# A decode block on one core: longer contiguous runs for K, V and w_down, and a softmax per chunk of keys in place of one per group

**Chip, cores, metric.** One core of one Trainium2 chip. All times are device microseconds of one execution; the kernel before takes 477 us. A program on one core has no second die to compare with, so I treat runs as comparable when they ran on the same chip in the same rounds.

## The reference

One token, model width 1024, everything in bf16:

```python
mod = silu(c) @ w_mod                      # 1024 x 6144 -> sa, ca, ga, sb, cb, gb
h = layernorm(x) * (1 + ca) + sa
x = x + ga * attention(h)                  # wq 1024x4096, 32 heads, 4 KV groups,
                                           # 65536 keys x 128, softmax, wo 4096x1024
h = layernorm(x) * (1 + cb) + sb
x = x + gb * ((gelu(h @ w_gate) * (h @ w_up)) @ w_down)   # 1024 -> 3584 -> 1024
```

What has to be loaded: w_mod 12.6 MB, wq 8.4, K and V 134.2, wo 8.4, gate and up 14.7, w_down 7.3: 185.6 MB in all, of which K and V are 72%.

## The kernel before

The engines go by their short names: PE is TensorE, DVE VectorE, ACT ScalarE, POOL GpSimd, and SP (SyncE) issues the loads. PSUM is the memory that PE writes.

K and V come in chunks of 8192 keys (2.097 MB), 8 chunks for each of the 4 groups, so 32 chunks of K and 32 of V. All loads are issued by SP, in one fixed order, into nine staging buffers of 2 MB; each load waits until PE has freed its buffer. For each K chunk PE transposes 128x128 blocks into PSUM, DVE and ACT take turns to evict them, and PE multiplies them with q. The scores of a whole group (65,536 keys) are kept, and the exponent waits for the group's maximum. V therefore follows K by LAG = 10 chunks. A step below is the work on one K chunk and one V chunk; a K-only step has no V chunk yet.

```python
E_KEYS = 16                                     # keys in one contiguous run: 16*128*2 B = 4 KB
CH = min(E_KEYS * P * 4, SK)                    # 8192 keys in a chunk
NA = CH // (P * E_KEYS)                         # 4 runs per partition
LAG = NCH + 2                                   # NCH = 8 chunks in a group
NKT = 8
NDD = 7                                         # row blocks of w_down in one load

def kv_src(tensor_ap, i):
    g, cch = divmod(i, NCH)
    return tensor_ap[0, g, cch * CH:(cch + 1) * CH, :].rearrange("(a p e) d -> p a (e d)", p=P, e=E_KEYS)
# ... cut ...
for st, (ki, vi) in enumerate(steps):           # order of the loads, vi = ki - LAG
    if ki is not None:
        ...                                     # K chunk, in kb0-kb2, wb0, wb1
    if vi is not None:
        addjob(("v", vi), f"vb{vi % 3}")        # V chunk, in three buffers
# ... cut: ACT, once per group ...
def emit_exp(g, h):
    if h == 0:
        wt(ac, s["dve"], ("negm_ready", g))     # the group's maximum
        wt(ac, sa, ("sccopied", g * NCH + NCH - 1))
    inst = ac.activation(out=PT[g % 2][:, h, :], in_=S[g % 2][:, h, :], func=ACT.Exp,
                         bias=negm[...], scale=SCALE, accum_out=sums[...])
# ... cut: PE ...
def emit_PV(vi, u):
    if u == 0:
        vbuf_t[vi] = job_begin(key)
        if cv == 0:
            wt(pe, s["exp"], ("exp_done", gv))  # first V chunk waits for the whole group
# ... cut: a buffer is freed by an instruction of its own ...
def job_end(key, inst=None):
    if inst is None:
        inst = pe.drain(fusable=True)
    rec(("free", key), b.fsem.inc(inst, 1))
```

Of the kernel before, what the change touches and what calls it, by code (L numbers as in the profile page):

```python
# [5 lines left out]
P = 128  # L6
# [6 lines left out]
E_KEYS = 16  # L13
STAGE_COLS = 8192

# [34 lines left out]
def bass_adaLN_cond__gqa_block_cached__geglu_ffn__decode_kernel(  # L50
# [26 lines left out]
    CH = min(E_KEYS * P * 4, SK)  # L77
    assert SK % CH == 0 and CH % (P * E_KEYS) == 0
    NA = CH // (P * E_KEYS)
    NB = NA * E_KEYS  # L80
# [3 lines left out]
    assert NCH >= 2  # L84
    NKC = G * NCH
    LAG = NCH + 2
    NSTEPS = NKC + LAG
    NKT = 8
    NTB = 4
    SLAG = 3  # L90
    SCALE = float(DH) ** -0.5
    EPS = 1e-5
    NBQ = SK // P
    WO_ROWS = HPG * DH
    NDD = 7
    assert CH <= STAGE_COLS

    with ExitStack() as es:
# [5 lines left out]
            "misc", "gp", "gpmx", "pe", "dve", "act", "t2act", "t2dve", "ea", "ed", "sdone", "scdone",  # L104
# [19 lines left out]
        S = [sb(f"S{j}", [P, HPG, NBQ], FP32) for j in range(2)]  # L124
        PT = [sb(f"PT{j}", [P, HPG, NBQ]) for j in range(2)]
# [16 lines left out]
        rmax = sb("rmax", [P, G * HPG], FP32)  # L142
        cmax = sb("cmax", [P, G * HPG], FP32)
        gmax = sb("gmax", [P, G * HPG], FP32)
        negm = sb("negm", [P, G * HPG], FP32)
        sums = sb("sums", [P, G * HPG], FP32)
# [18 lines left out]
        PVB = [pst("pv")]  # L165
        PR = [pst("pr")]
# [52 lines left out]
        pro_rot = ["kb0", "kb1", "kb2", "wb0", "wb1", "vb0", "vb1", "vb2"]  # L219
        kpool = ["kb0", "kb1", "kb2", "wb0", "wb1"]  # L220
# [10 lines left out]
        for st, (ki, vi) in enumerate(steps):  # L231
# [10 lines left out]
            if vi is not None:  # L242
                addjob(("v", vi), f"vb{vi % 3}")
                gq, cv = divmod(vi, NCH)
                if cv == WO_AT_CV:
                    addjob(("wo", gq), "wob")
                    s_last = v_step(gq * NCH + NCH - 1)
                    wo_step[gq] = (s_last + 2) if (s_last + 2) < NSTEPS else None
# [14 lines left out]
        pr_uses = []  # L263

        def prog_gp(gp):
# [9 lines left out]
            for g in range(G):  # L275
                wt(gp, s["dve"], ("rmax_ready", g))
                inst = gp.partition_all_reduce(gmax[:, g * HPG:(g + 1) * HPG], rmax[:, g * HPG:(g + 1) * HPG],
                                               P, bass.bass_isa.ReduceOp.max)
                rec(("gmax_ready", g), s["gpmx"].inc(inst, 1))

        def prog_sync(sy):
# [28 lines left out]
            for key, bname in jobs:  # L310
# [20 lines left out]
                elif kind == "down":  # L331
                    k0, k1 = down_jobs[key[1]]
                    src = B_w_down[k0 * P:k1 * P, :].rearrange("(ci p) n -> p ci n", p=P)
                    issue(key, lambda t, n=k1 - k0: t[:, 0:n * D].rearrange("p (ci n) -> p ci n", ci=n), src)
                else:
                    raise ValueError(key)
# [5 lines left out]
        def prog_pe(pe):  # L342
            pr = s["pr"]
            for b_ in BUFS.values():
                b_.consumed = 0

# [6 lines left out]
            def job_end(key, inst=None):  # L353
# [3 lines left out]
                if inst is None:  # L357
                    inst = pe.drain(fusable=True)
                rec(("free", key), b.fsem.inc(inst, 1))

            def pr_use(key):
                k = len(pr_uses)
                pr_uses.append(key)
                if k >= 1:
                    wt(pe, s["dve"], ("prfree", pr_uses[k - 1]))
                return 0, k

            def pr_done(key, inst=None):
                if inst is None:
                    inst = pe.drain(fusable=True)  # L370
                rec(("pr_ready", key), pr.inc(inst, 1))

            def matvec(prkey, lhs_fn, ncols, rhs_cols):
                bank, k = pr_use(prkey)
                last = None
                n = len(rhs_cols)
                for t in range(ncols):
                    for ci in range(n):
                        last = pe.matmul(PR[bank][:, t:t + 1], lhs_fn(ci, t), rhs_cols[ci],  # L379
                                         start=(ci == 0), stop=(ci == n - 1))  # L380
# [6 lines left out]
            inst = pe.matmul(PR[bank][:, 0:NI], x8[:, :], ident[0:NI, 0:NI], start=True, stop=True)  # L387
# [3 lines left out]
            inst = pe.matmul(PR[bank][:, 0:NI], silu8[:, :], ident[0:NI, 0:NI], start=True, stop=True)  # L391
# [9 lines left out]
            inst = pe.matmul(PR[bank][:, 0:1], ones_f[:, :], part1[:, 0:1], start=True, stop=True)  # L401
# [3 lines left out]
            inst = pe.matmul(PR[bank][:, 0:1], ones_f[:, :], part1[:, 1:2], start=True, stop=True)  # L405
# [7 lines left out]

            evac_done = {"act": s["ea"], "dve": s["ed"]}
# [5 lines left out]
            def emit_T(i, u):  # L420
# [5 lines left out]
                g, cch = divmod(i, NCH)  # L426
                tb = U % NTB
                ev = evac_engine(U)
                if U >= NTB:
                    Up = U - NTB  # L430
                    wt(pe, evac_done[evac_engine(Up)], ("evac_done", Up))
                last = None
                for bb in range(BU):
                    b = u * BU + bb
                    slot = blk_slot(b)
                    last = pe.matmul(TB[tb][:, bb * P:(bb + 1) * P], tt[:, slot:slot + P], ident[:, :],  # L436
                                     start=True, stop=True)
# [5 lines left out]
            def emit_S(i, u):  # L443
# [3 lines left out]
                if u == 0:  # L447
                    if i == 0:
                        wt(pe, s["dve"], "qT_ready")
                    if i >= 2:  # L450
                        wt(pe, s["act"], ("scfree", i - 2))
# [4 lines left out]
                for bb in range(BU):  # L456
                    b = u * BU + bb
                    last = pe.matmul(SC[scb][:, b * HPG:(b + 1) * HPG], kt[:, slot0 + bb * P:slot0 + (bb + 1) * P],  # L458
                                     qT[:, g * HPG:(g + 1) * HPG], start=True, stop=True)
                rec(("sdone", U), sdone.inc(last, 1))  # L460
                if u == NU - 1:
                    rec(("scdone", i), s["scdone"].inc(pe.drain(fusable=True), 1))  # L462
# [9 lines left out]
            def emit_PV(vi, u):  # L472
                key = ("v", vi)
                gv, cv = divmod(vi, NCH)
                if u == 0:
                    vbuf_t[vi] = job_begin(key)
                    if cv == 0:
                        wt(pe, s["exp"], ("exp_done", gv))
                        if gv >= 1:
                            wt(pe, s["dve"], ("pvfree", gv - 1))  # L480
                tt = vbuf_t[vi]
                last = None
                for bb in range(BU):
                    b = u * BU + bb
                    bq = cv * NB + b
                    slot = blk_slot(b)
                    first = (cv == 0 and b == 0)
                    final = (cv == NCH - 1 and b == NB - 1)
                    last = pe.matmul(PVB[0][:, 0:HPG], tt[:, slot:slot + DH], PT[gv % 2][:, :, bq],  # L489
                                     start=first, stop=final)  # L490
                if u == NU - 1:
                    job_end(key)
                    if cv == NCH - 1:
                        rec(("pv_done", gv), s["pv"].inc(pe.drain(fusable=True), 1))

            def group_tot(gv):
                wt(pe, s["exp"], ("exp_done", gv))
                bank, k = pr_use(("tot", gv))
                inst = pe.matmul(PR[bank][:, 0:HPG], ones_f[:, :], sums[:, gv * HPG:(gv + 1) * HPG],  # L499
                                 start=True, stop=True)  # L500
                pr_done(("tot", gv), inst)

            def group_wo(gv):
# [3 lines left out]
                bank, k = pr_use(("woacc", gv))  # L507
                last = None
                for t in range(NI):
                    for hl in range(HPG):  # L510
                        last = pe.matmul(PR[bank][:, t:t + 1],  # L511
                                         tt[:, hl * D + t * P:hl * D + (t + 1) * P],
                                         oT[:, gv * HPG + hl:gv * HPG + hl + 1],
                                         start=(hl == 0), stop=(hl == HPG - 1))
# [33 lines left out]

            wt(pe, s["dve"], "ln2_part1_ready")
            bank, k = pr_use("ln2_sum1")  # L550
            inst = pe.matmul(PR[bank][:, 0:1], ones_f[:, :], part1[:, 2:3], start=True, stop=True)
# [3 lines left out]
            inst = pe.matmul(PR[bank][:, 0:1], ones_f[:, :], part1[:, 3:4], start=True, stop=True)  # L555
            pr_done("ln2_sum2", inst)
            wt(pe, s["dve"], "h2T_ready")
            for kind in ("gate", "up"):
                for j2 in range(NI // 2):
                    key = (kind, j2)  # L560
                    tt = job_begin(key)
                    matvec((kind, j2), lambda ci, t, tt=tt: tt[:, ci * F + t * P:ci * F + (t + 1) * P],
# [3 lines left out]
            for jd, (k0, k1) in enumerate(down_jobs):  # L566
# [4 lines left out]
                job_end(key)  # L571
            wt(pe, s["dve"], "outT_ready")
            bank, k = pr_use("outT")
            inst = pe.matmul(PR[bank][0:NI, 0:P], outT_b[:, :], ident[:, :], start=True, stop=True)
            pr_done("outT", inst)

        def prog_dve(dv):
# [4 lines left out]

            def prbank(key):
                return PR[0]
# [106 lines left out]
            def chunk_max(i):  # L691
                g, cch = divmod(i, NCH)
                wt(dv, s["act"], ("sccopied", i))
                chain_wait()
                if cch == 0:
                    target = rmax[:, g * HPG:(g + 1) * HPG]
                else:
                    target = cmax[:, g * HPG:(g + 1) * HPG]
                inst = dv.tensor_reduce(out=target, in_=S[g % 2][:, :, cch * NB:(cch + 1) * NB], axis=AX.X,  # L699
                                        op=ALU.max)  # L700
                done(inst)
                if cch > 0:
                    chain_wait()
                    inst = dv.tensor_tensor(out=rmax[:, g * HPG:(g + 1) * HPG], in0=rmax[:, g * HPG:(g + 1) * HPG],
                                            in1=target, op=ALU.max)
                    done(inst)
                if cch == NCH - 1:
                    rec(("rmax_ready", g), sd.count)

            def group_negm(g):  # L710
                wt(dv, s["gpmx"], ("gmax_ready", g))
                inst = dv.tensor_scalar(out=negm[:, g * HPG:(g + 1) * HPG], in0=gmax[:, g * HPG:(g + 1) * HPG],  # L712
# [258 lines left out]
```

## Time and profile before

| | us |
|---|---|
| median of 16 runs (beside those of the changed kernel) | 477.05 |
| lowest to highest | 475.95 to 481.90 |
| span of the profiled execution | 476.0 |
| mean granted clock of TensorE | 0.713 |

The lines themselves are in the prediction below. The page cuts the span into 40 slices of 11.9 us and gives for each the busy share of every engine in tenths, the granted clock of TensorE and what the DMA engines moved. A table of stretches gives the same counters between two times of one's choice. Read the DMA share together with GB/s: a full share at a low rate means that the transfers themselves are slow; a low share means that some engines had nothing left to carry, mostly because nothing was queued.

### The profile page before, as it was taken

The numbers are of one execution on the slowest core, as the hardware profiler recorded it, in microseconds if no ns is written. First come the engines' busy times: TensorE is split into PE (matmuls) and PEld (weight loads), VectorE is DVE, ScalarE is ACT, GpSimd is POOL, SyncE is SP. The second block draws the span as 40 slices with busy tenths as digits, with TensorE's granted clock in tenths as the row PEclk, the third lists the DMA queues.
The fourth block names the chain that finished last, engine by engine and source line by source line (L and its number), as shares of the span: only waits on it lengthen the run. The fifth ranks groups of instructions, "written<-read, shape, count | busy, mean of one in ns | idle before, by whom it ended". The sixth has DMA issues, their size and how long they took to land.

```text
span 476.0 us, 17150 instructions
## 1 busy us (share of the span) xinstructions
PE 341.9 (72%) x7731; PEld 322.6 (68%) x7731; DVE 210.8 (44%) x400; ACT 207.0 (43%) x361; POOL 2.3 (0%) x11
## 2 busy tenths in 40 slices
PE   0445398888598989989889988999989553164242
PEld 0344287777498989988879988899979442154232
DVE  0002078888476675545465565445755000020010
ACT  2000077787965565675355567545655500010000
POOL 0000000000000000000000000000000000000000
PEclk9999999999788685556585575565887555555555
DMA  8999999999989999999999999999998999999994
GB/s 316 423 421 421 410 408 407 406 410 406 408 346 352 394 407 398 407 408 408 407 408 407 400 405 407 408 409 390 399 368 305 412 409 405 404 418 418 409 386 159
DMA packets 46201, 186.71 MB, mean 392 GB/s; under 512 B 1584, under 2 KB 1584, under 8 KB 44080
## 3 DMA queue, kind: packets, MB, share of 16 engines
q1 hardware_dynamic: 46128, 185.61, 98.1%
q8 instruction: 61, 1.00, 0.9%
q14 instruction: 12, 0.10, 0.1%
HBM read 185.60 MB, written 0.00 MB: 390 GB/s over the span
## 4 chain that ended last, share of the span: by engine, by line
PE 38%; issue 23%; DMA 20%; SPq 8%; ACT 6%; DVE 3%; PEldq 0%; PEld 0%; POOLq 0%; POOL 0%; DVEq 0%; ACTq 0%
PE tb L436 23%; SPq L297 8%; PE sc L458 7%; PE pv L489 6%; DMA vb<-in_w_mod_dram 6%; DMA vb<-in_A_v_cache_dram 6%; DMA kb<-in_B_w_down_dram 4%; DMA kb<-in_A_k_cache_dram 4%; ACT PT L883 3%; ACT kt L862 3%; DVE kt L688 1%; DVE cmax L699 1%; PE pr L511 1%; PE pr L379 1%; ACT L883 0%
## 5 line engine op out<-in xcount | busy, mean ns | idle before, releaser
L688 DVE CAST kt<-tb 128x512 bf16<-128x512 f32 x256 | 174.9, 690 | 109.8 <-PE tb L436 109.5
L862 ACT ACTIVATE kt<-tb 128x512 bf16<-128x512 f32 x256 | 151.6, 600 | 128.9 <-PE tb L436 126.6
L489 PE MATMUL pv<-PT,vb 128*128 128x8 bf16 x2048 | 119.8, 180 | 34.9 <-DMA vb<-in_A_v_cache_dram 20.8
L489 PEld LDWEIGHTS pv<-PT,vb 128*128 128x128 bf16 x2048 | 111.6, 111 | 41.5 <-DMA vb<-in_A_v_cache_dram 23.0
L458 PE MATMUL sc<-qT,kt 128*128 128x8 bf16 x2048 | 126.7, 167 | 18.1 <-ACT kt L862 8.3
L436 PE MATMUL tb<-ident,kb 128*128 128x128 bf16 x1152 | 132.0, 254 | 7.3 <-DMA kb<-in_A_k_cache_dram 4.2
L458 PEld LDWEIGHTS sc<-qT,kt 128*128 128x128 bf16 x2048 | 95.6, 100 | 24.3 <-ACT kt L862 11.2
L436 PE MATMUL tb<-ident,wb 128*128 128x128 bf16 x704 | 90.7, 275 | 1.4 <-issue 0.3
L436 PEld LDWEIGHTS tb<-ident,kb 128*128 128x128 bf16 x1152 | 81.0, 110 | 9.5 <-DMA kb<-in_A_k_cache_dram 4.3
L436 PEld LDWEIGHTS tb<-ident,wb 128*128 128x128 bf16 x704 | 54.4, 118 | 2.5 <-issue 2.0
L872 ACT ACTIVATE S<-sc 128x512 f32<-128x512 f32 x32 | 33.8, 1058 | 4.7 <-PEq L462 4.2
L883 ACT ACTIVATE PT<-S,negm 128x512 bf16<-128x512 f32 x32 | 22.6, 709 | 1.6 <-DVE negm L712 1.6
L920 ACT ACTIVATE stat<-stat 128x1 f32<-128x1 f32 x1 | 0.2, 203 | 47.3 <-DVE stat L643 47.3
L718 DVE RECIPROCAL rtot<-pr 128x8 f32<-128x8 f32 x4 | 0.8, 208 | 43.2 <-PE pr L499 43.2
L699 DVE TENSOR_REDUCE cmax<-S 128x8 f32<-128x512 f32 x28 | 18.9, 676 | 2.3 <-ACT S L872 2.3
L436 PE MATMUL tb<-ident,vb 128*128 128x128 bf16 x192 | 16.3, 217 | 0.3
L850 ACT ACTIVATE stat<-stat 128x1 f32<-128x1 f32 x1 | 0.2, 203 | 35.3 <-DVE stat L643 35.3
L923 ACT ACTIVATE ff<-ff 128x28 f32<-128x28 f32 x1 | 0.2, 226 | 29.3 <-DVE ff L810 29.3
L379 PE MATMUL pr<-h2T,vb 128*128 128x1 bf16 x168 | 5.0, 165 | 9.5 <-DMA vb<-in_B_w_up_dram 9.5
L436 PEld LDWEIGHTS tb<-ident,vb 128*128 128x128 bf16 x192 | 11.1, 96 | 0.6 <-issue 0.6
L379 PE MATMUL pr<-ffT,kb 128*128 128x1 bf16 x168 | 5.0, 165 | 9.0 <-DMA kb<-in_B_w_down_dram 9.0
L616 DVE TENSOR_TENSOR modacc<-modacc,pr 128x48 f32<-128x48 f32 x7 | 1.4, 204 | 22.5 <-PE pr L379 22.5
(103 smaller groups left out, 126.2 us busy)
## 6 DMA issues: line engine op xcount, KB each, us to landing
vb<-in_A_v_cache_dram SPq DMA_DIRECT2D x32, 2048.0 KB, 13.3
kb<-in_A_k_cache_dram SPq DMA_DIRECT2D x18, 2048.0 KB, 21.8
wb<-in_A_k_cache_dram SPq DMA_DIRECT2D x11, 2048.0 KB, 22.5
wob<-in_A_wo_dram SPq DMA_DIRECT2D x4, 2048.0 KB, 17.9
vb<-in_A_k_cache_dram SPq DMA_DIRECT2D x3, 2048.0 KB, 25.4
kb<-in_B_w_gate_dram SPq DMA_DIRECT2D x3, 1792.0 KB, 20.1
vb<-in_B_w_up_dram SPq DMA_DIRECT2D x3, 1792.0 KB, 29.9
kb<-in_B_w_down_dram SPq DMA_DIRECT2D x3, 1792.0 KB, 20.6
```

What stands on the lines that cost most here:

```text
L297: inst = sy.dma_start(dst_fn(b.t), src_ap)
L379: last = pe.matmul(PR[bank][:, t:t + 1], lhs_fn(ci, t), rhs_cols[ci], start=(ci == 0), stop=(ci == n - 1))
L436: last = pe.matmul(TB[tb][:, bb * P:(bb + 1) * P], tt[:, slot:slot + P], ident[:, :], start=True, stop=True)
L458: last = pe.matmul(SC[scb][:, b * HPG:(b + 1) * HPG], kt[:, slot0 + bb * P:slot0 + (bb + 1) * P], qT[:, g * HPG:(g + 1) * HPG], start=True ...
L489: last = pe.matmul(PVB[0][:, 0:HPG], tt[:, slot:slot + DH], PT[gv % 2][:, :, bq], start=first, stop=final)
L511: last = pe.matmul(PR[bank][:, t:t + 1], tt[:, hl * D + t * P:hl * D + (t + 1) * P], oT[:, gv * HPG + hl:gv * HPG + hl + 1], start=(hl == ...
L616: inst = dv.tensor_tensor(out=modacc[:, :], in0=modacc[:, :], in1=prbank(("mod", i))[:, 0:NT_MOD], op=ALU.add)
L688: inst = dv.tensor_copy(kt[:, slot0:slot0 + BU * P], TB[tb][:, 0:BU * P])
L699: inst = dv.tensor_reduce(out=target, in_=S[g % 2][:, :, cch * NB:(cch + 1) * NB], axis=AX.X, op=ALU.max)
L862: inst = ac.activation(out=kt[:, slot0:slot0 + BU * P], in_=TB[tb][:, 0:BU * P], func=ACT.Copy)
L872: inst = ac.activation(out=out_ap, in_=in_ap, func=ACT.Copy)
L883: inst = ac.activation(out=PT[g % 2][:, h, :], in_=S[g % 2][:, h, :], func=ACT.Exp, bias=negm[:, g * HPG + h:g * HPG + h + 1], scale=SCALE ...
```

## The change

Its intent is to make the loads faster and to keep them coming. Cut to the core:

```diff
-    CH = min(E_KEYS * P * 4, SK)
-    NA = CH // (P * E_KEYS)
-    NB = NA * E_KEYS
+    CH = min(CHUNK_KEYS, SK)          # 8192, as before
+    E_KEYS = CH // P                  # 64 keys in a run: 16 KB
+    NA = 1
+    NB = E_KEYS
-    LAG = NCH + 2
+    LAG = 3
-    NKT = 8
+    NKT = 6
-    NDD = 7
+    NDD = 8
-    kpool = ["kb0", "kb1", "kb2", "wb0", "wb1"]
+    kpool = ["kb0", "kb1", "kb2", "wb0"]
+    vpool = ["vb0", "vb1", "vb2", "wb1"]
 # w_down: eight rows of 2 KB that follow each other in memory go to one partition, 16 KB in a run
-    src = B_w_down[k0 * P:k1 * P, :].rearrange("(ci p) n -> p ci n", p=P)
+    src = B_w_down[k0 * P:k1 * P, :].rearrange("(p ci) n -> p (ci n)", ci=k1 - k0)
 # so gate and up must deliver their columns in that order: stationary reads with a step of n elements
+    def ff_cols(tt, ci, t):
+        n = k1 - k0
+        lo = ci * F + k0 * P + (t - k0)
+        return tt[:, lo:lo + (P - 1) * n + 1:n]
 # softmax per chunk: maximum from PSUM, all-reduce, x - max with a transposing write, exp, sum
+    def chunk_max(i):      dv.tensor_reduce(rmax[i], SC[i % 2] as "p h b", max)
+    def chunk_negm(i):     dv.tensor_scalar(negm[i], gmax[i], -1.0)       # after POOL's all-reduce
+    def chunk_sc_copy(i):  dv.tensor_tensor(SR[i % 2] as "p b h", SC[i % 2], negm[i], add)
+    def emit_exp(i, h):    ac.activation(PTR[i % 4], SR[i % 2], Exp, scale=SCALE)
+    def chunk_psum(i):     dv.tensor_reduce(sums[i], PTR[i % 4], add)
 # ... cut: group_post weights the 8 chunks of a group by exp(their max - the group's max) and adds them
 # PE: free a buffer with an increment on the next matmul, no drain
     def job_end(key, inst=None):
-        if inst is None:
-            inst = pe.drain(fusable=True)
-        rec(("free", key), b.fsem.inc(inst, 1))
+        definc(b.fsem, ("free", key), inst)      # waits in a list until the next mm()
```

Small matrix-vector results now rotate over the PSUM banks GB and TB instead of using one bank.

## The prediction

> **What bounds the kernel now.** I read the page's slices first, then the DMA queues, then the same counters over chosen stretches, then the order of time inside one step. The slices:
>
> ```profile
> PE   0445398888598989989889988999989553164242
> PEclk9999999999788685556585575565887555555555
> DMA  8999999999989999999999999999998999999994
> GB/s 316 423 421 421 410 408 407 406 410 406 408 346 352 394 407 398 407 408 408 407 408 407 400 405 407 408 409 390 399 368 305 412 409 405 404 418 418 409 386 159
> DMA packets 46201, 186.71 MB, mean 392 GB/s; under 512 B 1584, under 2 KB 1584, under 8 KB 44080
> ```
>
> The DMA row is full from end to end, and 186 MB in 476 us is nearly all that this core moves at its best slice (423 GB/s). So the transfers set the time. PE reads 9 in the middle, but there it runs at half clock. Two things in this view are worth money: the rate differs between stages although DMA is equally "busy" in each, and there are dips (slices 12-13 and 28-31). I then asked for the stretches one by one; columns are stretch, length, busy us of PE, PEld, DVE, ACT, POOL, clock, DMA share, GB/s:
>
> ```profile
> 12.00:36.00 24.00, 10.14 (x346) 9.60 (x342) 1.43 (x7) 0.00 (x0) 0.00 (x0) 1.00 1.01 423
> 108.00:120.00 12.00, 10.36 (x231) 9.36 (x227) 10.29 (x18) 9.68 (x16) 0.00 (x0) 1.00 1.02 408
> 140.00:144.00 4.00, 3.68 (x96) 3.39 (x93) 3.09 (x6) 2.14 (x5) 0.00 (x0) 1.00 0.38 132
> 264.00:276.00 12.00, 11.79 (x218) 11.44 (x216) 6.89 (x11) 6.18 (x11) 0.00 (x0) 0.50 1.04 400
> 364.00:368.00 4.00, 3.43 (x101) 3.10 (x99) 1.91 (x3) 2.54 (x4) 0.00 (x0) 1.00 0.55 177
> 372.00:418.00 46.00, 17.70 (x579) 16.76 (x579) 0.54 (x3) 4.98 (x13) 0.00 (x0) 0.50 1.03 407
> 426.00:444.00 18.00, 9.38 (x330) 9.02 (x326) 0.92 (x5) 0.00 (x0) 0.00 (x0) 0.50 1.01 418
> 456.00:468.00 12.00, 4.54 (x159) 4.40 (x159) 0.33 (x3) 0.00 (x0) 0.00 (x0) 0.50 1.04 384
> ```
>
> At a full share the rate is 423 while w_mod loads (12 KB contiguous per partition), 418 for gate and up (7 KB), 407 to 408 for K and V (4 KB), 384 for w_down (2 KB). The rate follows the run length, not the engines: 372 to 418 has PE at 38% and still 407. The two starved stretches are 140 to 144 (all buffers full: the first group's softmax had to wait for eight chunks of K) and 364 to 368.
>
> **What the Trainium skill says.** "DMA: Bandwidth & Descriptors", section "Why small descriptors are slow (HBM only)", names a fixed overhead per packet. The trace agrees: one fixed cost fits all four rates. An engine carries 1/16 of the rate: 12288 B take 465 ns at 423, 4096 B take 160.6 ns at 408. The difference gives 0.0371 ns per byte and 8.5 ns per packet; from these 7 KB should run at 417 (418 seen) and 2 KB at 388 (384 seen). The same page, "Where 436 GB/s comes from", puts the ceiling at 435; my fit's limit for endless runs is 431. "Advanced Engine Details and Errata", section "SBUF Cachelines", says that an access to a new 16-byte line each time pays a penalty. The change makes the stationary reads of gate and up step by 16 bytes. No stationary operand of the kernel before is strided, so its trace says nothing here. "TensorE: Matmul & The Clock Gate", "What's actually happening", gives two clock states, 4/8 and 8/8; the stretches above at 0.50 and 1.00 agree.
>
> **The change part by part.** (1) *Longer runs.* K and V chunks go from 16 keys (4 KB) to 64 keys (16 KB) per partition in one run; w_down's rows are regrouped so that eight 2 KB rows become one 16 KB run. By the fit a 16 KB packet takes 8.5 + 608 = 617 ns, 425 GB/s. K and V are 64 x 2.097 = 134.2 MB: 329.0 us at 408, 315.8 at 425, so 13.2 us less. w_down is 7.34 MB: 19.1 us at 384, 17.3 us at about 424 (its last job has 8 KB runs), 1.8 us less. As DMA is the bound, both count in full: -15.0 us.
>
> (2) *Softmax per chunk instead of per group.* Each chunk of 8192 keys gets its own maximum, exponent and sum, combined at the group's end, so V follows K by 3 steps and not by 10. The long K-only lead that fills all buffers and then starves the queue disappears, and so does the end where the last group's exponents hold everything back. Lost now, measured against 407 GB/s: 136 to 148 lose 0.25 + 2.7 + 0.45 = 3.4 us; 328 to 332, 344 to 348 and 364 to 368 lose 0.5 + 0.5 + 2.3 = 3.3 us. Of these 6.7 us I give 2 to new waits: -4.7 us.
>
> (3) *What it adds, beside the path if the engines have room.* DVE per chunk now: eight evictions at 0.69, one maximum of 0.68 and 0.17 = 6.4 us. After: 8 x 0.69, a maximum straight from PSUM (estimate 0.7), negation 0.17, the subtraction that writes with a stride (estimate 1.1, because ACT's strided copy of the same 128x512 takes 1.06 against 0.60 for a plain one), a sum of 0.68: 8.2 us. ACT loses the 1.06 copy and the accumulator reads (0.19 each): 8 x 0.60 + 0.71 = 5.5 us. The all-reduce on POOL takes 0.37 us, 32 times instead of 4, with one eviction between request and use. A step of one K and one V chunk takes DMA 2 x 2.097 MB / 425 = 9.9 us, so DVE at 8.2 stays hidden. Only the three first K-only steps will run at DVE's pace, about 8 us each; eight staging buffers cover that.
>
> (4) *PE.* Same matmuls. In the order of time at half clock one unit (4 transposes, 4 of PV, 4 scores) repeats every 0.64 us:
>
> ```profile
> 257.54 0.69 DVE L688 CAST kt<-tb 128x512 bf16<-128x512 f32 x1 [0.47 <-PE tb L436]
> 257.56 0.59 PE L436 MATMUL tb<-ident,wb 128*128 128x128 bf16 x4
> 257.94 0.30 PE L489 MATMUL pv<-PT,vb 128*128 128x8 bf16 x4
> 258.09 0.25 PE L458 MATMUL sc<-qT,kt 128*128 128x8 bf16 x4
> 258.20 0.59 PE L436 MATMUL tb<-ident,wb 128*128 128x128 bf16 x4
> ```
>
> 16 x 0.64 = 10.24 us a step; the output projection adds 1.9 us in 8 steps: 10.5 us. DMA per step after: 9.87 + one 2.097 MB load of wo per 8 steps at 388 GB/s, 0.68: 10.55 us. So at half clock PE has just enough room, at full clock plenty. The drains that now signal freed buffers and finished scores (bubbles of 0.2 to 0.4 us two or three times a step) are replaced by an increment on the next matmul, which is what makes 10.24 reachable.
>
> (5) *End.* From the last landing to the end now takes 4.75 us; the chain shows where it begins:
>
> ```profile
> 452.72 18.53 DMA kb<-in_B_w_down_dram
> 471.30 1.66 PE pr L379 x56
> 472.99 0.17 DVE down_acc L828
> ```
>
> w_down goes from 4 x 7 to 8 + 8 + 8 + 4 row blocks, so the last job has 32 matmuls instead of 56, at 29.5 ns each: -0.7 us. The rotation of PSUM banks frees PE from waiting for each small eviction; with DMA the bound that is worth nothing.
>
> Sum: 477.2 - 15.0 - 4.7 - 0.7 = 456.8, say **457 us**.
>
> **The rivals.** *PE or DVE becomes the bound.* For it: margin at half clock is 0.05 us a step, and DVE's new strided work may delay evictions that PE needs. Against it: before runs at 0.62 mean clock in the middle, not 0.50, and four PSUM banks give PE 2.5 us of slack. If a step took 11.0 us, 29 steps would be 319 against 306 us, less about 5 us of lead: some 465 us. *The rate does not follow the run length* (16 KB no better than 4 KB): then only parts 2 and 5 remain, 472 us, "same". Against it: four rates on one line, two of them not used for the fit. *Strided weight loads in gate and up.* 448 weight loads, now about 29.5 ns each (56 in 1.65 us). They have from h2T, about 10 us after the last V chunk lands (416.2 to 425.7 now), until the weights end 52 us after it; less 4 us for the activation chain and 6 us for the first three down jobs this leaves 32 us, 71 ns per matmul. Twice as slow (59 ns) is still hidden; at 90 ns it adds 8 us (465), at four times some 21 us (478). Nothing in the profile decides between these; I give over 71 ns a chance of one in five.
>
> **Range and chances.** The rivals reach 465 from two sides, and a few us of stall that I keep might vanish (452); a fit limit of 431 leaves little below 449. Range 449 to 468. 2% faster is 467.7: only a failed rate gain or a fourfold weight load miss it. Faster 0.84, within 2% 0.13, slower 0.03.
>
> **What would show it.** Part 1: K and V stretches at 422 to 426 GB/s with a full share, packets down from 46201 to about 18,500 (24,576 fewer for K and V, 3,072 fewer for w_down). Part 2: no slice under 380 before the last. Part 3: per-step DVE near 8.2 us, subtraction near 1.1, DVE idle mostly on PE. Part 4: PE idle on DMA of K or V, not on DVE. Part 5: the chain ends with a w_down landing. I am wrong if the rate stays at 408 with a full share, if the DMA share falls in the middle with PE at 98%, or if gate and up loads run over 71 ns each and the chain's end goes through them.

## The result

| | median us | lowest to highest | runs | clock of the profiled run |
|---|---|---|---|---|
| before | 477.05 | 475.95 to 481.90 | 16 | 0.713 |
| after | 458.23 | 457.93 to 458.48 | 11 | 0.761 |

The ratio is 0.9591 (95% interval 0.9567 to 0.9615): faster by 4.1%, 19.5 us of 477. Here and below a ratio is the mean time of one kernel's runs over that of the other's of the same rounds, so it is not quite the ratio of the medians. Executions over 1.5% slower than the fastest of the same kernel are left out of the means. Predicted were 457.0 us; the median is 1.2 us above.

The changed kernel is not only faster but steadier: its 11 runs lie within 0.55 us, the 16 runs before within 6.

The page of the changed kernel, cut to five of its lines; each slice is now 11.4 us:

```profile
PE   1335378888888398888968799887588888659754
PEclk9999999987787658867676959687677867555555
DMA  7999999999999999999999999999999999999992
GB/s 306 419 424 421 426 429 423 420 428 426 421 422 409 428 424 426 420 426 428 406 420 430 422 422 429 425 413 414 424 428 425 424 426 364 412 419 418 425 384 104
DMA packets 18553, 186.71 MB, mean 409 GB/s; under 512 B 1584, under 2 KB 1584, under 8 KB 7728
```

From the fifth to the thirty-third slice the rate is now what it was only under w_mod before. The two deep dips (346, 352 and 368, 305) are gone; small ones stay (409, 406, 413), and one of 364. The packets fell by 27,648, just the 24,576 of K and V and 3,072 of w_down that the prediction counted, and the bytes are the same.

Stretches of the changed kernel (stretch, length, busy us of PE, PEld, DVE, ACT, POOL, clock, DMA share, GB/s):

```profile
60.00:120.00 60.00, 50.58 (x1144) 48.15 (x1142) 49.12 (x81) 37.26 (x63) 2.22 (x6) 0.91 1.01 424
148.00:320.00 172.00, 142.22 (x3167) 138.58 (x3164) 119.08 (x209) 83.49 (x145) 5.84 (x16) 0.74 1.01 422
384.00:388.00 4.00, 2.46 (x46) 2.46 (x46) 1.98 (x4) 1.65 (x3) 0.00 (x0) 0.63 0.91 352
440.00:446.00 6.00, 2.84 (x100) 2.77 (x101) 0.50 (x3) 0.00 (x0) 0.00 (x0) 0.50 0.74 313
446.00:456.00 10.00, 4.04 (x131) 3.60 (x127) 1.27 (x7) 0.00 (x0) 0.00 (x0) 0.50 0.24 95
```

K and V run at 424 early and at 422 over the whole middle, wo included, with a full share. PE has 142 busy us in 172, so it waits. The last two lines show something that the prediction has not: the share falls to 0.74 from 440 on although every load has been issued. I come back to it.

The groups (line, engine, operation, count, busy us, mean ns, idle time before and its cause), then the waits (us in total, times, longest):

```profile
L764 DVE CAST kt<-tb 128x512 bf16<-128x512 f32 x256 | 172.4, 685 | 95.5 <-PE tb L493 94.7
L786 DVE TENSOR_TENSOR SR<-sc,negm 128x512 f32<-128x512 f32 x32 | 33.1, 1034 | 0.1
```

```profile
PE gb L366 <- DMA wb<-in_A_v_cache_dram: 19.0, 5, 4.5
PE gb L366 <- DMA vb<-in_A_v_cache_dram: 12.7, 8, 3.2
PE sc L366 <- DVE kt L764: 4.5, 9, 1.2
```

PE waits 31.7 us for V to land and only 4.5 us for an eviction by DVE. DVE in turn is idle for 95 us, because PE has no new transposes for it. The end of the chain of work that ended last, in order of time (start, us, what):

```profile
415.47 3.11 PE gb L366 x55
418.71 33.60 DMA kb<-in_B_w_down_dram
452.36 0.99 PE tb L366 x31
```

The last w_down load lands at 452.35; 4.1 us later the kernel is over (4.75 before). Gate's strided matmuls are on the inferred chain, but from 418.71 on it is the landing that counts.

### The profile page after: what moved, and what is told of

It reads as the page before. It is cut to its first block, busy times and chain, and to the rows that moved or that the text cites. A ratio compares the mean times of both kernels' runs of the same rounds, so it can differ in the third digit from the quotient of the medians.

```text
span 456.5 us, 17156 instructions
## 1 busy us (share of the span) xinstructions
PE 337.5 (74%) x7731; PEld 327.1 (72%) x7731; DVE 253.4 (56%) x488; ACT 176.8 (39%) x301; POOL 12.6 (3%) x39
## 4 chain that ended last, share of the span: by engine, by line
DMA 49%; PE 31%; SPq 11%; DVE 4%; issue 4%; ACT 1%; DVEq 0%; ACTq 0%
DMA wb<-in_A_v_cache_dram 31%; PE tb L366 15%; SPq L314 11%; DMA kb<-in_B_w_down_dram 7%; DMA wb<-in_w_mod_dram 7%; PE gb L366 6%; DMA kb<-in_A_k_cache_dram 4%; PE tb L493 4%; PE sc L366 4%; PE sc L516 1%; PE gb L546 1%; DVE kt L764 1%; DVE rmax L770 1%; DVE SR L786 0%; ACT kt L967 0%
## 5 line engine op out<-in xcount | busy, mean ns | idle before, releaser
L366 PE MATMUL tb<-ident,kb 128*128 128x128 bf16 x1152 | 153.4, 256 | 11.2 <-DMA kb<-in_A_k_cache_dram 8.3
L366 PE MATMUL sc<-qT,kt 128*128 128x8 bf16 x1536 | 112.7, 167 | 12.5 <-issue 5.5
L366 PE MATMUL gb<-PTR,vb 128*128 128x8 bf16 x1152 | 90.9, 180 | 15.8 <-DMA vb<-in_A_v_cache_dram 12.7
L493 PE MATMUL tb<-ident,kb 128*128 128x128 bf16 x384 | 100.7, 262 | 0.0
L366 PEld LDWEIGHTS gb<-PTR,vb 128*128 128x128 bf16 x1152 | 79.9, 110 | 17.9 <-DMA vb<-in_A_v_cache_dram 14.3
L366 PEld LDWEIGHTS sc<-qT,kt 128*128 128x128 bf16 x1536 | 78.7, 99 | 14.9 <-issue 5.6
L366 PEld LDWEIGHTS tb<-ident,kb 128*128 128x128 bf16 x1152 | 79.0, 107 | 11.7 <-DMA kb<-in_A_k_cache_dram 8.6
L516 PE MATMUL sc<-qT,kt 128*128 128x8 bf16 x512 | 85.3, 167 | 0.0
L546 PE MATMUL gb<-PTR,vb 128*128 128x8 bf16 x384 | 65.1, 175 | 2.1 <-issue 2.0
L516 PEld LDWEIGHTS sc<-qT,kt 128*128 128x128 bf16 x512 | 50.7, 99 | 3.0 <-issue 3.0
L493 PEld LDWEIGHTS tb<-ident,kb 128*128 128x128 bf16 x384 | 46.9, 122 | 0.3 <-issue 0.3
L366 PE MATMUL gb<-PTR,wb 128*128 128x8 bf16 x384 | 31.2, 183 | 19.5 <-DMA wb<-in_A_v_cache_dram 19.0
L366 PEld LDWEIGHTS gb<-PTR,wb 128*128 128x128 bf16 x384 | 29.6, 120 | 20.7 <-DMA wb<-in_A_v_cache_dram 20.3
L546 PEld LDWEIGHTS gb<-PTR,vb 128*128 128x128 bf16 x384 | 37.9, 99 | 0.1
L786 DVE TENSOR_TENSOR SR<-sc,negm 128x512 f32<-128x512 f32 x32 | 33.1, 1034 | 0.1
L366 PEld LDWEIGHTS tb<-ident,wb 128*128 128x128 bf16 x384 | 25.1, 103 | 2.0 <-issue 2.0
```

The source lines that it names most:

```text
L366: inst = pe.matmul(*args, **kwargs)
L493: last = f(TB[tb][:, bb * P:(bb + 1) * P], tt[:, slot:slot + P], ident[:, :], start=True, stop=True)
L516: last = f(SC[scb][:, b * HPG:(b + 1) * HPG], kt[:, slot0 + bb * P:slot0 + (bb + 1) * P], qT[:, g * HPG:(g + 1) * HPG], start=True, stop=True)
L546: last = f(GB[gv % 2][:, cv * HPG:(cv + 1) * HPG], tt[:, slot:slot + DH], PTR[vi % NPR][:, :, b], start=first, stop=final)
L786: inst = dv.tensor_tensor(out=out_ap, in0=in_ap, in1=negm_b, op=ALU.add)
```

## The experiments

a_run4k, b_run16k, a_olddown and a_drains ran on one chip (before: 477.91 us median); a_lag6, a_3plus3, a_nostride_wrong and a_stride4 (before 478.66); a_gates2, a_gates3_ndd4, a_run8k and a_fetch (before 478.81). Each ratio is to the kernel before on the same chip. All ran, and all were correct except the one that is wrong on purpose. Where two kernels are set against each other, I take the difference of these ratios times 477 us; a ratio's interval is some 2 us to either side, so differences of 1 or 2 us are estimates.

### Does the run length make the rate? a_run4k and a_run8k

The changed kernel with only the run length of K and V set back to 4 KB, or to 8 KB with 32 in place of 16:

```diff
-    E_KEYS = CH // P
-    NA = 1
-    NB = E_KEYS
+    E_KEYS = 16
+    NA = CH // (P * E_KEYS)
+    NB = NA * E_KEYS
```

> The changed kernel with one thing undone: K and V are again read in runs of 4 KB per partition (16 keys) instead of 16 KB (64 keys); softmax per chunk, buffers, w_down stay as changed. Theory (the rate follows the run length): K and V stretches fall from 424 to about 408 GB/s at a full DMA share, the time rises by 134.2 MB/408 - 134.2 MB/424 = 12.4 us, to about 470.6 us (ratio to the kernel before 0.986). Rival (the higher rate comes from the deeper queue and the missing K-only lead, not from the runs): rate stays near 422, time 458 to 460 us (ratio 0.96).

> The changed kernel with K and V in runs of 8 KB, a third point for the cost of a packet. From 8.5 ns per packet and 0.0371 ns per byte on each engine: 419 GB/s in K and V stretches, 134.2 MB/419 - 134.2 MB/425 = 4.5 us more than with 16 KB, 462.7 us. If the cost were not per packet but a threshold between 4 and 16 KB, the time would be at either end, 458 or 471.6 us.

4 KB: 471.61 us (4 runs, 471.45 to 471.75), ratio 0.9862 [0.9808, 0.9916]. 8 KB: 462.76 us (4 runs, 462.54 to 462.86), 0.9669 [0.9636, 0.9702]. The same stretch as above, first at 4 KB, then at 8 KB:

```profile
60.00:120.00 60.00, 52.03 (x1124) 49.47 (x1125) 48.11 (x79) 36.53 (x62) 2.23 (x6) 0.86 1.03 407
```

```profile
60.00:120.00 60.00, 50.97 (x1144) 48.33 (x1144) 49.18 (x81) 37.27 (x63) 2.22 (x6) 0.91 1.01 419
```

The share is full in all three and the rate is 407, 419, 424. The prediction's line (0.0371 ns per byte and engine, 8.5 ns per packet) was drawn through 4 KB and 12 KB; at 8 KB it gives 8192 B in 312.4 ns, 16 engines 419.6 GB/s, and 419 was measured. So the run length alone is worth 0.0271 of 477 us between 4 KB and 16 KB: 12.9 us.

### Are long runs enough? b_run16k

The kernel before with 16 KB runs and nothing else, so with its group softmax, its LAG of 10 and its drains:

```diff
-E_KEYS = 16
+E_KEYS = 64
-    CH = min(E_KEYS * P * 4, SK)
+    CH = min(E_KEYS * P, SK)
```

> The kernel before with one thing done: K and V in runs of 16 KB per partition; softmax per group of eight chunks, buffers and w_down as before. Theory: rate in K and V stretches 424 GB/s; 12.6 us less if all of it counts, 464.5 us (ratio 0.974); but the K-only lead runs at 6.9 us a chunk on PE, DVE and ACT whatever the DMA does, so the queue starves earlier and longer after it and 2 to 4 us are given back: 465 to 468 us. Together with a_run4k this makes a two by two table; if the parts simply add, (before - a_run4k) is what the new softmax and w_down bring alone, about 6 us. Rival (run length without effect): 476 to 478 us.

474.73 us (14 runs, 470.53 to 480.75, one of them slow), ratio 0.9913 [0.9882, 0.9944]: 4.2 us, not the 9 to 12 that I expected. The rate is there, 424 GB/s from 60 to 120 us, but the queue runs dry for longer. Stretches, and SP's issues in order of time (start, us, what):

```profile
140.00:144.00 4.00, 4.00 (x85) 4.00 (x83) 2.78 (x6) 2.02 (x4) 0.00 (x0) 0.59 0.00 0
144.00:148.00 4.00, 3.79 (x103) 3.53 (x100) 2.81 (x5) 2.89 (x6) 0.00 (x0) 1.00 0.39 86
```

```profile
122.07 0.33 SPq L297 DMA_DIRECT2D kb<-in_A_k_cache_dram  x1
145.61 0.33 SPq L297 DMA_DIRECT2D vb<-in_A_v_cache_dram  x1
```

SP issues a K chunk at 122.07 and then nothing for 23.5 us, because the next V buffer is not free before the first group's softmax is done and the first V chunk consumed. In the kernel before the same hole lies between 121.50 and 142.67. The eight buffers that hold K and V (wob takes no K or V) last less long when they arrive faster, and PE, which has to end the wait, is no faster: it is busy all through these 8 us, in part at half clock. Over 132 to 148 and 328 to 372 us this run moves 164 and 352 GB/s and so loses 9.8 and 7.5 us against 424. Over the same two stretches the kernel before moves 321 and 362 GB/s and loses 3.4 and 4.9 us against 407 (the 6.7 of the prediction count only some pieces of them). That is 9 us more, enough to account for what the long runs did not bring (12.9 - 4.2 = 8.7).

With a_run4k this makes a square, in us gained over before, from the ratios:

| | one softmax per group | one softmax per chunk, w_down in 16 KB |
|---|---|---|
| K and V in 4 KB runs | 0 | 6.6 (a_run4k) |
| K and V in 16 KB runs | 4.2 (b_run16k) | 19.5 (after) |

The corners of one change alone add to 10.8; both together give 19.5. The 8.7 us between are the point: the long runs are worth 12.9 us only where the queue stays fed. The 8.7 us rest on three ratios, so they are uncertain by some 3 us.

### Is it the short lead that keeps the queue fed? a_lag6

The changed kernel, but V follows K by 6 chunks:

```diff
-    LAG = 3
+    LAG = 6
-    NPR = 4
+    NPR = 8
```

> The changed kernel with V following K by 6 steps instead of 3 (8 buffers for the exponents instead of 4, so that these don't limit it); everything else as changed. Theory (it is the length of the K-only lead against eight staging buffers that starves the queue): the sixth K step ends near 102 us, the loads run out near 90 us because the next V chunks need buffers that K chunks still hold; a dip of 5 to 8 us of transfer between 85 and 110 us that is never regained: 463 to 466 us (ratio 0.972). Rival (the lead is harmless with long runs; the gain of the new softmax lies elsewhere, in the last group's exponents or the drains): 457 to 460 us.

466.70 us (4 runs, 466.14 to 467.37), ratio 0.9753 [0.971, 0.9796], 0.016 or 7.7 us behind the changed kernel in its own rounds (0.9591). The starvation comes back, and only for want of buffers, as the softmax is still per chunk:

```profile
88.00:92.00 4.00, 3.58 (x82) 3.16 (x79) 4.00 (x8) 2.40 (x5) 0.37 (x1) 1.00 0.05 16
```

```profile
66.31 0.33 SPq L314 DMA_DIRECT2D kb<-in_A_k_cache_dram  x1
94.52 0.33 SPq L314 DMA_DIRECT2D vb<-in_A_v_cache_dram  x1
```

SP stands for 28 us. DVE is busy all of 88 to 92: in K-only steps it sets the pace. From 84 to 100 us the run loses 8.4 us against 424 GB/s, and it ends 7.7 us behind: the loss is not regained. So a lead of 3 chunks is covered by the eight staging buffers, as the prediction said (six do as well, in a_3plus3 below), and a lead of 6 is not. No run has the long lead with 4 KB runs in the changed kernel.

### w_down's long runs: a_olddown

The changed kernel with w_down as before (seven row blocks, 2 KB runs) and plain columns of gate and up:

```diff
-    NDD = 8
+    NDD = 7
-    src = B_w_down[k0 * P:k1 * P, :].rearrange("(p ci) n -> p (ci n)", ci=k1 - k0)
+    src = B_w_down[k0 * P:k1 * P, :].rearrange("(ci p) n -> p ci n", p=P)
-    return tt[:, lo:lo + (P - 1) * n + 1:n]
+    lo = ci * F + t * P
+    return tt[:, lo:lo + P]
```

> The changed kernel with w_down as before: four jobs of seven row blocks, 2 KB runs, and gate and up weights read by PE without stride. Theory (my sum): +1.8 us of transfer and +0.7 us for 24 more matmuls after the last landing: 460.7 us; gate and up groups of 56 matmuls back at 1.65 us from 3.28 us, with no effect on the end. Rival (the 16 KB runs of w_down or the strided loads cost at the end: in the changed kernel the DMA share falls to half from 442 us on while the last landing comes at 452 us): 455 to 457 us, and a share that stays above 0.9 until about 2 us before the last landing.

460.32 us (6 runs, 459.94 to 460.59), ratio 0.9627 [0.959, 0.9663]: 0.0036 or 1.7 us behind the changed kernel (2.1 by the medians). The prediction has 1.8 + 0.7 = 2.5 for this part. In this kernel too the share drops to 0.38 over the last 10 us, so the drop does not come from w_down's long runs.

### What the drains cost: a_drains

Every increment that waits for the next matmul is done by a drain at once, as before:

```diff
-    pend_incs.append((sem_, key_))
+    rec(key_, sem_.inc(pe.drain(fusable=True), 1))
```

> The changed kernel with PE's drains put back: buffer frees and finished scores are signalled by a drain instead of an increment on the next matmul. Theory (transfers are the bound and PE has room, mean clock 0.74 in the middle): within 1.5 us of 458.2 us. Rival (PE at half clock has only 0.05 us per step of room, as my prediction put it): about 0.5 us of bubbles per step times 29 steps, less some 5 us of lead: 465 to 470 us, and a DMA share below 1.0 in the middle.

459.73 us (458.96 to 462.11), ratio 0.962 [0.958, 0.966]: 0.0029 or 1.4 us behind the changed kernel, and the intervals overlap. Over a stretch of the middle:

```profile
120.00:240.00 120.00, 105.51 (x2090) 100.42 (x2088) 79.46 (x135) 55.33 (x96) 4.04 (x11) 0.64 1.01 422
```

The share is full and the rate 422 in spite of the drains, so in the middle they do not set the pace: the margin of 0.05 us a step is for a step at half clock throughout, and the middle had a clock of 0.74 (0.64 here). At the end they do, in the profiled run (460.5 us, one of the slower of the six). By its marks in the trace the last load lands at 452.0, no later than in the changed kernel (452.3), but PE is behind: gate's first pass starts at 418.15 in place of 409.02, the eight strided passes of gate and up then follow each other with gaps of 0.3 us, and the chain that ended last runs over PE (start, us, what):

```profile
443.02 3.26 PE tb L366 x55
454.62 0.97 PE tb L366 x31
```

The last products start 2.3 us later than in the changed kernel, and the two profiles' spans differ by 2.2 us. So the rival "PE becomes the bound" is true of the end of this run; without the drains the strided passes have the room that hides them.

### The strided weight loads: a_nostride_wrong and a_stride4

The first reads gate's and up's columns without a step, so its result is wrong (relative error 0.17). The second has four row blocks per w_down load, so a step of 8 bytes in place of 16:

```diff
# a_nostride_wrong
-    return tt[:, lo:lo + (P - 1) * n + 1:n]
+    lo = ci * F + t * P
+    return tt[:, lo:lo + P]
# a_stride4
-    NDD = 8
+    NDD = 4
```

> The changed kernel with gate and up weights read by PE without stride while w_down keeps its regrouped rows: the order of the hidden units no longer matches, so the result is wrong on purpose; all work and all waits are the same. It takes the cost of the strided weight loads by itself. Theory (they take twice as long, 58.6 instead of 29.5 ns per matmul, but lie under the transfers): groups of 56 at 1.65 us, time 457.5 to 458.5 us. Rival (the strided loads delay the activation and so the first w_down products near 440 us): 454 to 456 us.

> The changed kernel with w_down in seven jobs of four row blocks: 8 KB runs, and weight loads of gate and up that step by 8 bytes instead of 16. Theory (the Trainium skill's 16-byte lines): two columns share a line, so the load is as fast as without stride, 1.65 us per group of 56. Rival (any step costs[...]): 3.28 us per group as with 16 bytes. The time stays within 1 us of 458.2 us in both, w_down at 419 instead of 424 GB/s being worth 0.2 us.

458.12 us (6 runs), 0.9574 [0.9541, 0.9607], and 458.89 us (6 runs), 0.9589 [0.9555, 0.9622]: neither differs from the changed kernel. The order of time on PE (start, us, what; each matmul loads 128 weight columns and multiplies one column), first in the changed kernel, then with 8 bytes, then without a step:

```profile
412.19 3.25 PE L366 MATMUL tb<-h2T,kb 128*128 128x1 bf16 x55
415.34 3.25 PE L366 MATMUL gb<-h2T,kb 128*128 128x1 bf16 x55
```

```profile
408.97 1.99 PE L366 MATMUL tb<-h2T,kb 128*128 128x1 bf16 x55 [1.56 <-DVE h2T L736]
410.85 0.91 PE L366 MATMUL tb<-h2T,kb 128*128 128x1 bf16 x23
```

```profile
408.81 1.62 PE L366 MATMUL tb<-h2T,kb 128*128 128x1 bf16 x55 [1.56 <-DVE h2T L737]
410.33 1.42 PE L366 MATMUL tb<-h2T,kb 128*128 128x1 bf16 x48
```

From start to start one pass is 56 matmuls (55 and one that closes the job): 3.15, 1.88 and 1.52 us, so 56, 33.6 and 27.1 ns each, all at a clock of 0.50. A step of 16 bytes doubles the time per matmul, one of 8 bytes adds 24%, which neither side of the expectation for a_stride4 had: the penalty exists, it is graded, and in the changed kernel it costs nothing, since 56 is under the 71 ns that the prediction worked out. In a_drains, where PE starts these passes 9.1 us later, it is not hidden.

### What sets the end? a_3plus3, a_gates2, a_gates3_ndd4 and a_fetch

A transfer is carried by sixteen engines, and each reports its part. By those sixteen marks in the trace, the parts of one load of the changed kernel land within 0.7 us of each other at the start and within 9.6 us at the end (3.0 before): that fits the falling share of 440 to 456. In outline two theories were put to the first three of these runs. A: the most loaded engine has no gaps, so it sets the end, and evening out the others' landings changes nothing. B: the spread is itself lost time, which comes from stalls or from a deep queue, and can be won back.

a_3plus3 makes the queue less deep: three K and three V buffers in place of four and four.

```diff
-    kpool = ["kb0", "kb1", "kb2", "wb0"]
+    kpool = ["kb0", "kb1", "kb2"]
-    vpool = ["vb0", "vb1", "vb2", "wb1"]
+    vpool = ["vb0", "vb1", "vb2"]
```

a_gates2 queues two loads of gate ahead of V chunks 29 and 30, so that the dip at 380 to 388, where the last V chunks find all buffers taken, has something to carry. a_gates3_ndd4 does so with three, and takes w_down in loads of four row blocks.

```diff
     if vi is not None:
+        if 0 <= vi - (NKC - 3) < 2:          # 3 in a_gates3_ndd4
+            addjob(("gate", vi - (NKC - 3)), kpool[vi - (NKC - 3)])
         addjob(("v", vi), vpool[vi % len(vpool)])
```

a_fetch asks whether POOL's traffic for instructions loads one DMA engine more than the others: 120 waits that are already satisfied are added after each of the 32 all-reduces.

```diff
     rec(("gmax_ready", i), s["gpmx"].inc(inst, 1))
+    for _ in range(120):
+        wt(gp, sp, "gp_ready")
```

> The changed kernel with three buffers for K and three for V instead of four and four. Question: in the changed kernel the sixteen parts of the last transfers land 9.6 us apart and the DMA share halves 10 us before the last landing; before they landed 3 us apart. Theory A (one DMA engine has more work than the others and sets the end in any case; a deep queue only lets the others run ahead): parts land closer together, but the last landing comes no earlier: 458 to 463 us, the excess over 458.2 being new waits for buffers. Theory B (the deep queue itself makes the spread, and it costs): last landing earlier, 454 to 456 us.

> The changed kernel with the first two loads of gate weights queued before the last but two and the last but one V chunk, into K buffers that are free by then. In the changed kernel the queue waits there for V buffers, and the mean DMA share falls to 0.86 to 0.91 between 380 and 388 us, some 1.5 us of transfer. Theory A (the most loaded DMA engine, some 10 us behind the first one, sets the end; it has work in this dip too): the dip goes, the time stays at 458.0 to 458.6 us. Theory C (every dip of the mean share counts): 456.4 to 457.0 us, which would also be a version faster than both kernels.

> As the run with two early gate loads, but three of them, and w_down in seven jobs of 8 KB runs, so that gate and up products take 1.9 us a group instead of 3.1 us and PE has room for the later start of the MLP. Theory A: 458.0 to 459.0 us. Theory C: 456 to 457 us.

> The changed kernel with 120 waits on a semaphore that has long been reached put after each all-reduce on POOL: no work, only some 3800 more instructions to fetch. The DMA view shows 61 packets of 1.00 MB for instructions, 0.9% of all engines' span, 66 us of one engine, 1.08 us each. Theory A' (unevenly spread instruction fetches are what makes one DMA engine the last): some 15 more fetch packets, and the last landing 1 to 10 us later, depending on which engines they fall. Rival (they fall on engines with slack, or the spread has another cause): 458.0 to 458.6 us.

| | median us (runs) | ratio, interval | spread of the last load's landings, us |
|---|---|---|---|
| after (other rounds) | 458.23 (11) | 0.9591 [0.9567, 0.9615] | 9.6 |
| a_3plus3 | 458.67 (6) | 0.9592 [0.9554, 0.9631] | 3.3 |
| a_gates2 | 458.47 (6) | 0.9584 [0.9553, 0.9614] | 3.6 |
| a_gates3_ndd4 | 461.01 (4) | 0.9633 [0.96, 0.9665] | 1.6 |
| a_fetch | 458.24 (5) | 0.9577 [0.9548, 0.9607] | 8.6 |

a_3plus3 keeps its share full to 448, eight us longer than the changed kernel, and still its last w_down products start at the same time. A stretch and the last step of its chain:

```profile
444.00:448.00 4.00, 1.87 (x64) 1.79 (x64) 0.16 (x1) 0.00 (x0) 0.00 (x0) 0.50 0.98 414
```

```profile
452.29 0.98 PE tb L366 x31
```

a_gates2 fills the dip, 403 GB/s where the changed kernel has 352, and starts its last products at 452.46:

```profile
384.00:388.00 4.00, 3.10 (x80) 3.10 (x80) 2.62 (x6) 2.42 (x4) 0.00 (x0) 0.89 0.98 403
```

Both even out the landings by some 6 us and gain nothing: the last part lands at 452.2 and 452.4, against 452.3 in the changed kernel. That is what theory A expects; that one engine has no gaps is not shown. Nor is the depth of the queue what makes the spread: a_drains, with all eight buffers, has 3.5 us. What they save at one place reappears as lower slices elsewhere (325 and 388 in a_3plus3; 355, 388 and 363 in a_gates2). a_gates3_ndd4 went too far: the three early gates delay the last V chunk (it lands at 411.87), with it the whole second half, and the queue has nothing free to fill: its DMA share from 400 to 440 is 0.86, at 352 GB/s. Here the last landing itself comes 2.5 us later (454.8), and 461.01 us lies outside what both theories expected. a_fetch gives 458.24 us, the same as the changed kernel; the queue that carries POOL's instructions went from 12 packets to 27, the 15 more that were expected, and they hardly load an engine. Why the parts land so far apart stays open. The records don't tell the engines of one transfer apart well enough to say which is the loaded one.

## Why the prediction was right, step by step

**The bound.** Right: the share is full, K and V run at 424, and PE and DVE wait for DMA or for each other's next input.

**Step 1, longer runs of K and V.** Predicted 13.2 us, measured 12.9 (after against a_run4k). The line through four rates held for two lengths that it had not seen, 8 KB (419) and 16 KB (424 for 425). For w_down with the shorter last job: 2.5 predicted, 1.7 measured (after against a_olddown).

**Step 2, softmax per chunk.** Predicted 4.7, measured 4.9: a_run4k gains 6.6 in all, of which 1.7 belong to w_down. So the three terms came to 12.9 + 1.7 + 4.9 = 19.5 against a predicted 20.4, with no term far off. The 4.9 is what the other two leave: it holds the softmax together with the drains, the PSUM banks and the new split of the buffers, and no run takes the softmax alone. Within it, the 2 us kept for new waits were a guess that happened to fit: the dips from 376 to 392 us (400, 348, 352 and 400 GB/s) lose 1.9 us. And the sum hides a condition that the prediction didn't name. It added the two parts as if each stood alone. They don't: long runs alone give 4.2 us (b_run16k), as with a long lead a faster queue empties sooner and then waits the longer. The sum came out because its order happens to be the right one, with the stalls priced at the old rate and the runs at the new schedule; the prediction gives no reason for that order, so this part is luck.

**Step 3, DVE and ACT.** Per chunk DVE now has 8 x 0.685 + 0.681 + 0.162 + 1.034 + 0.675 = 8.0 us (8.2 predicted), ACT 8 x 0.594 + 0.63 = 5.4 (5.5); the subtraction takes 1.03 us, 1.1 predicted from ACT's strided copy. The Trainium skill's "VectorE: DVE Perf Modes", section "The TRN2 errata — SBUF-src ops pay a fixed extra latency per instruction", would give 691 ns for a plain 512-element fp32 addition; the trace has 1034, so the estimate by a like strided instruction in the trace was the better one. The K-only steps ran at 7.1 and 7.0 us with DVE busy all the time, so it paces them, but faster than the 8 I gave it. The whole chain runs in them already; the records of neighbouring instructions overlap (a maximum of 0.68 us starts at 68.22, the next eviction at 68.82), so that the 8.0 summed from single durations is too long.

**Step 4, PE.** The mechanism holds in the middle (PE waits for V to land), but there the drains were not what made it reachable: with them the middle still runs at 422 (a_drains). What their removal buys lies at the end, which the prediction did not see: with drains PE sets it, at a cost of 1.4 us by the ratios and 2.2 between the two profiles. The margin of 0.05 us a step is right for half clock and too narrow a picture for a clock of 0.74.

**Step 5, end.** 4.1 us from the last landing, 4.05 predicted. The chain ends with a w_down landing, as said.

**Claims that failed.** "No slice under 380 before the last": slice 34 has 364. wo's last load with its 2 KB runs lies there, and the dip at 380 to 388, where the share falls to 0.86 and 0.91. The runs show that filling the dip brings nothing (a_gates2). The share that falls from 440 on was not foreseen; no run here removes this tail and gains, so I don't call it the cause of the 1.2 us by which the median misses.

**The rivals.** That the rate doesn't follow the run length: refuted by a_run4k and a_run8k. That PE or DVE becomes the bound: refuted for the changed kernel; b_run16k shows it in the kernel before, where PE is busy through the hole that the group's softmax makes, and a_drains at its end. That strided loads cost time: they double, and stay hidden as long as PE is not late for them (a_drains).

**Steadiness.** Within one call the fast runs of the kernels with a group softmax spread over 5 to 6 us (before 4.6 to 6.3, b_run16k 5.9), those of the changed one over 0.6 (its variants up to 3.2, a_drains). A stall whose end PE sets should move with PE's clock, and the record leans that way: over the 13 fast runs of b_run16k the time rises by some 1 us for each 0.01 that the mean clock falls (0.759 to 0.719, correlation -0.62), over those of the changed kernel by 0.14 us. No run held the clock fixed, so this stays an argument.

## What to carry to other kernels

In a kernel that is bound by its loads, tabulate GB/s at a full DMA share against the contiguous bytes per partition of each load: two lengths give a fixed cost per packet, and the rest can be worked out. A faster load pays only if something is always queued, so compare the lead in chunks with the buffers before adding up gains, and two such changes can be worth more together than apart, as here. At the end of such a kernel look at the landing of the last part, not at the mean share; filling a dip in the mean need not move the end.

## What the Trainium skill lacked or had wrong

- "DMA: Bandwidth & Descriptors", sections "Specifications" and "Measured (HBM→SBUF, 128 partitions, SWDGE, issued from GpSimd)": they give 512 B as the smallest transfer at line rate and otherwise rate a DMA by its total size. Here all large loads are of 1 to 2 MB with runs far over 512 B, and the rate still goes with the run: 384 GB/s at 2 KB (before), 407 at 4 KB, 419 at 8 KB, 424 at 16 KB. From 4 to 16 KB this is worth 12.9 us of 471.
- Same page, section "Why small descriptors are slow (HBM only)": it holds concatenation of descriptors worth it only at 256 B or less. The fixed cost fitted here is 8.5 ns per packet and engine, 5% of a 4 KB packet's 160.6 ns. (Here the runs were made longer; concatenation itself was not tried.)
- Same page: it has the sixteen engines of a transfer finish independently, but doesn't say how far apart the parts can land. Here the last load's parts landed over 9.6 us, and 3.0 in the kernel before, and evening them out (3.3) didn't move the end.
- "Advanced Engine Details and Errata", section "SBUF Cachelines": it asks for two hits on a line and gives no size of the penalty. Measured for 128-column weight loads with one-column matmuls at half clock: 27.1 ns without a step, 33.6 at 8 bytes (two elements in each 16-byte line, so not quite free), 56 at 16 bytes.
- "VectorE: DVE Perf Modes": 691 ns for an fp32 tensor_tensor of 512 elements; 1034 ns here, with a PSUM source, a broadcast operand and an output step of 256 bytes. No run separates the three, so the figure is not shown to be wrong. A reduction of the same PSUM tile with a strided read took 681 ns, no longer than the 676 of one from SBUF before.
- No page says what a step in the run length does to a kernel with a lead: 4.2 us alone, 12.9 us with the shorter lead.
